# Dividing the first batch's softmax weights: by a diagonal in TensorE's turn, or row by row on GpSimd

## The chip, the cores and the metric

The kernel runs on one core of one Trainium2 chip. A core has five engines that run side by side, each with its own queue of instructions: TensorE (PE; its weight loads are listed as PEld) multiplies matrices into PSUM, VectorE (DVE) and ScalarE (ACT) work element by element and can read PSUM, GpSimd (POOL) works element by element in SBUF and issues some of the DMAs, SyncE (SP) issues the other DMAs. An engine takes its instructions strictly in order; a semaphore holds it where it needs another's result.

The metric is the device time of one execution in microseconds. The time before is 1459.56 us, the median of 3 runs (1455.29 to 1461.54).

## What is computed

A threshold attention, and behind it a two-layer block with the exact GELU. The attention keeps in each row only the scores that lie within tau of the row's largest, takes their exponentials, divides each row by its sum plus 1e-9, and weighs V with the result:

```python
batch, n_heads, seq, head_dim = (8, 8, 576, 64)            # q, k, v in FP32, tau = 0.02
scores = scale * np.matmul(q, k.transpose(0, 1, 3, 2))
thresh = np.max(scores, axis=-1, keepdims=True) - tau
scores = np.where(scores >= thresh, scores, -1000000000.0)
scores = scores - np.max(scores, axis=-1, keepdims=True)
attn = np.exp(scores)
attn = attn / (np.sum(attn, axis=-1, keepdims=True) + 1e-09)
attn_out = np.matmul(attn, v)
x = attn_out.transpose(0, 2, 1, 3).reshape(B * S, H * D)   # 4608 x 512
h = x @ w_in                                               # 512 x 2048
g = 0.5 * h * (1.0 + erf(h * inv_sqrt2))
out = g @ w_out                                            # 2048 x 512
```

`w_in` and `w_out` arrive in 64-bit floating point and are converted to FP32 by the kernel itself. Everything is computed in FP32.

## The kernel before

The heads are taken two at a time: a pair p is two heads of one batch, four pairs to a batch, 32 in all. The 576 rows of a pair's scores are cut into four chunks of 128 rows for each head and a fifth chunk that holds the last 64 rows of both heads. One pair and one chunk make a slot. A slot of chunk 0 to 3 works on two heads (n = 2 in the code, e = 0 and 1), a slot of chunk 4 on one tile. The main loop (L796) walks the slots, and within a slot the instructions of all engines are written out by hand in a fixed order; no scheduler reorders them.

Batch 0 (p below EARLY = 4) has 20 slots and is walked in two passes: chunks 0 and 1 of the four pairs (slots 0 to 7), then chunks 2, 3 and 4 of each pair (slots 8 to 19). What a slot of batch 0 does, in the order of the loop:

- `scores` (L351, matmuls L360): scores into the two PSUM buffers of the tag "sc". Each buffer comes free when the slot before has masked its scores (L391).
- `softmax_head` (L363): for each head the row maximum on DVE (L372, `nmx`), the threshold on POOL (L373, `thr`), the exponentials on ACT (L375, into `w`, a tile named p).
- `gelus`, `weigh_v`, `fill`, `table`: from slot 9 on, a part of the two-layer block's matmuls (L524) fills TensorE, and ACT does their GELUs (L503), which need another function table than the exponential: a table load before, and one behind (L510). `weigh_v` (L466) multiplies the turned weights with V, and ACT copies the result (L482).
- `turn_p_early` (L294) of the slot before: TensorE turns the 128x576 weights of each head, in 128-column pieces (L304) and 64-column remainders (L306), into PSUM buffers of the tag "mm" (four, shared with all other matmuls), and ACT copies them out (L314, L324; for chunk 4 DVE, L317 and L329).
- `softmax_tail` (L378): DVE sets to zero what is under the threshold and sums the rest in one instruction (L391), which needs scores, threshold and exponentials. POOL adds 1e-9 to the sum of each head (L394).
- `turn_qk_early` (L262) in slots 0, 2 and 4: Q and K of the next pair are turned.
- the conversions and the division. `conversions` (L162) turns the 32 pieces of the two weight matrices from 64 bits to FP32: on DVE `expo` (L179), `mant` (L186), `power` (L188) and the product (L190), on ACT `power` (L180); then `load_piece` (L140) lets POOL issue two DMAs (L157, L159) for a further piece. `convert(ns)` issues conversion steps until a debt of so many nominal nanoseconds is paid: 0 in slot 0, 3400 in slots 1 to 7, 3650 in slots 8 to 18, all that is left in slot 19. Of this share, 700 ns come first; then `divide_early` (L398): a reciprocal of the sums on DVE (L402), and on POOL one multiplication of a head's 128x576 weights by it, in place (L405); then the rest of the share.

So the next slot's thresholds (L373) stand on POOL behind this slot's multiplications and behind the DMA issues of this slot's pieces, and the next slot's maxima (L372) stand on DVE behind this slot's conversions.

From batch 1 on, weights are turned by DVE and DMAs and the division is done on the product with V (`divisors`, L407); the SBUF buffer of its divisors has the tag "inv" in the pool `dg`, one buffer. TensorE has the two-layer block to work on in all the time that attention leaves.

Of the kernel before, what the change touches and what calls it, by code (L numbers as in the profile page):

```python
# [8 lines left out]
FP32 = mybir.dt.float32  # L9
U32 = mybir.dt.uint32  # L10
U8 = mybir.dt.uint8
AF = mybir.ActivationFunctionType
ALU = mybir.AluOpType
# [5 lines left out]
def kernel(  # L19
# [28 lines left out]
    nc = tc.nc  # L48
    ctx.enter_context(tc.manual_schedule())

    B, H, S, D = q.shape
    d_model, d_ff = moe_w_in.shape
    P = 128
    Q = 32
    HP = H // 2
    NP = B * HP
    EARLY = HP
# [28 lines left out]
    dg = ctx.enter_context(tc.tile_pool(name="dg", bufs=1))  # L86
# [5 lines left out]
    ident = const.tile([P, P], FP32, name="ident")  # L92
# [105 lines left out]
    def convert(ns):  # L198

        if conv["steps"] is None:  # L200
            conv["steps"] = conversions()
        conv["debt"] += ns
        while conv["debt"] > 0:
            took = next(conv["steps"], None)
            if took is None:
                return
            conv["debt"] -= took
# [85 lines left out]

    def turn_p_early(p, i):  # L294

        s = st[p]
        if i == 0 or (p < HP and i == 2):
            s["pT"] = [one.tile([P, KR, S], FP32, tag=f"pT{e}", name=f"pT{e}") for e in range(2)]
        w = s.pop(("p", i))
        n = 1 if i == NC else 2  # L300

        def turn(to, cols, e):
            if cols.stop - cols.start == P:
                nc.tensor.transpose(to, w[:, cols], ident)  # L304
            else:
                nc.tensor.matmul(to, lhsT=w[:, cols], rhs=ident, start=True, stop=True)  # L306

        for e in range(n):
            tr = ps.tile([P, NC, P], FP32, tag="mm", name="tr")
            for c in range(NC):  # L310
                at = e * (S + TAIL) + c * P
                turn(tr[:, c, :], slice(at, at + P), e)
            if i < NC:
                nc.scalar.copy(s["pT"][e][:, 0:NC, i * P:(i + 1) * P], tr)  # L314
        if i == NC:
            for e in range(2):
                nc.vector.tensor_copy(s["pT"][e][:, 0:NC, MAIN:S], tr[:, :, e * TAIL:(e + 1) * TAIL])  # L317
        tails = s["pT"][0][:, NC, :]
        tr = ps.tile([P, NC, P], FP32, tag="mm", name="tr")
        if i < NC:  # L320
            for e in range(2):
                at = MAIN + e * TAIL
                turn(tr[e * TAIL:(e + 1) * TAIL, 0, :], slice(at, at + TAIL), e)
            nc.scalar.copy(tails[:, i * P:(i + 1) * P], tr[:, 0, :])  # L324
            return
        turn(tr[0:TAIL, 0, :], slice(MAIN, S), 0)
        for e in range(2):
            rows = slice(e * TAIL, (e + 1) * TAIL)
            nc.vector.tensor_copy(tails[rows, MAIN:S], tr[0:TAIL, 0, rows])  # L329
# [21 lines left out]
    def scores(p, i):  # L351
        s = st[p]
        n = 1 if i == NC else 2
        sc = s["sc", i] = [ps.tile([P, 2, 512], FP32, tag="sc", name="sc", bufs=2) for _ in range(n)]
        for h in range(2):
            for e in range(n):
                rows = slice(0, P) if i == NC else slice(e * D, (e + 1) * D)
                lhsT = s["q_tail"] if i == NC else s["qT"][rows, i * P:(i + 1) * P]
                at = h * HALF + (TAIL if p < EARLY and e == 0 else 0)
                nc.tensor.matmul(  # L360
                    sc[e][:, h, 0:HALF], lhsT=lhsT, rhs=s["kT"][rows, at:at + HALF], start=True, stop=True)
# [16 lines left out]
    def softmax_tail(p, i):  # L378

        s = st[p]  # L380
        sc, thr, w = s.pop(("sc", i)), s.pop(("thr", i)), s["p", i]
        n = len(sc)
        if p < EARLY:
            pair = small.tile([P, 2], FP32, tag="den", name="den")
            den = [pair[:, e:e + 1] for e in range(n)]
        else:
            at = [e * NC + i if i < NC else 2 * NC for e in range(n)]
            den = [sums[p % 2][:, x:x + 1] for x in at]
        for e in range(n):
            row = w[:, e * S:(e + 1) * S].rearrange("p (h s) -> p h s", h=2)  # L390
            nc.vector.scalar_tensor_tensor(  # L391
                row, sc[e][:, :, 0:HALF], thr[:, e:e + 1], row, op0=ALU.is_ge, op1=ALU.mult, accum_out=den[e])
            if p < EARLY:
                nc.gpsimd.tensor_scalar(den[e], den[e], 1e-9, None, op0=ALU.add)  # L394
        if p < EARLY:
            s["sum", i] = pair[:, 0:n]

    def divide_early(p, i):  # L398

        s = st[p]  # L400
        den, w = s.pop(("sum", i)), s["p", i]
        nc.vector.reciprocal(den, den)  # L402
        for e in range(den.shape[1]):
            row = w[:, e * S:(e + 1) * S]
            nc.gpsimd.tensor_scalar(row, row, den[:, e:e + 1], None, op0=ALU.mult)  # L405

    def divisors(p):  # L407

# [89 lines left out]
    def gelus(left):  # L498

        while len(late) > left:  # L500
            g, j, hT = late.pop(0)
            t = gp.tile([P, 2, TOK], FP32, tag="g", name="g")
            nc.scalar.activation(t, hT, AF.Gelu)  # L503
            g[j - 1], g[j] = t[:, 0, :], t[:, 1, :]
            dirty[0] = True
# [270 lines left out]
    BATCH = HP * SLOTS  # L776
# [19 lines left out]
    for n in range(len(slots) + WEIGH + 1):  # L796
        p, i = slots[n] if n < len(slots) else divmod(n, SLOTS)
        early = p < EARLY
        last = slots[n - 1] if 0 < n <= len(slots) else None
        if p < NP:  # L800
            scores(p, i)
            softmax_head(p, i)
        elif n == len(slots):
            ext = weights_in()
        if not early or n % 2 == 0:
            gelus(0)
            table()
        made = []
        for args in due:
            weigh_v(*args)  # L810
        due = []
        if p > EARLY and i == WEIGH:
            made = [weigh_v(p - 1, h * HALF, (h + 1) * HALF) for h in range(2)]
        owed += (goal(n) - goal(n - 1)) * BLK_NS * (PARTS[i] if not early and p < NP else 1.0)
        if early:
            fill(owed, tokens)
            owed = 0.0
            table()
        if last and last[0] < EARLY and last[1] < NC:
            turn_p_early(*last)  # L820
        if p < NP:
            softmax_tail(p, i)
        if made:
            made[0]()
        if p < NP and not early:
            turn_p(p, i)
        if made:
            made[1]()
        if p < NP and not early:
            if i == 2:  # L830
                regroup(p, 1)
            if i > 2:
                regroup(p, i)
            if i == NC:
                divisors(p)
        if last and last[0] < EARLY and last[1] == NC:
            turn_p_early(*last)
        if p < HP - 1 and i == 0:
            turn_qk_early(p + 1)
            if p == 0:  # L840
                load_early(3)
                load_v_early(2)
                load_v_early(3)
            if p < 2:
                load_piece()
        if p < HP and i == NC and 0 < p < HP - 1:
            load(p + 3)
        if n == BATCH:
            for t in pd_tail:
                nc.gpsimd.memset(t[:, NB:4 * KR, :], 0.0)  # L850
        if p >= HP and i == 1 and p + 2 < NP:
            loads = load_steps(p + 2)
        if p >= HP:
            next(loads, None)
        if p >= HP - 1 and i == 2 and p + 1 < NP:
            turn_qk(p + 1)
        share = 0 if n == 0 else 3400 if n < 2 * HP else 3650 if n < BATCH - 1 else 1e9
        if early:
            convert(min(share, 700))
            divide_early(p, i)  # L860
            share -= min(share, 700)
        convert(share)
        if not early:
            lag[0] = 2 if p < NP else 0
            fill(owed, tokens)
            owed = 0.0
        if last and last[0] < EARLY:
            if last[1] == 1:
                due.append((last[0], 0, TOK))
            if last[1] == NC:  # L870
                due.append((last[0], TOK, S))
        if n == START - 1:
            tokens = TOK
        elif n == BATCH + 1:
            tokens = S
        elif p > EARLY and i == WEIGH and p % HP == 0:
            tokens = p // HP * S
            for n in AWAY:
                if n in x_blk and (n + 1) * TOK <= tokens:
                    put_away(n)  # L880
# [34 lines left out]
```

## Time and profile before

| | |
|---|---|
| median of 3 runs | 1459.56 us (1455.29 to 1461.54) |
| the profiled execution: its own time, and its span | 1455.29 us, 1453.4 us |
| busy in the span: PE, DVE, ACT, POOL | 1386.1, 908.4, 629.2, 463.2 us |
| busy in the first 192 us: PE, DVE, ACT, POOL | 141.0, 141.9, 104.3, 139.7 us |
| L405 on POOL (weights times reciprocal) | 36, 76.1 us |
| L304 on PE (transposes of 128 columns) | 144, 26.2 us |
| L306 on PE (64-column remainders, as matmuls) | 72 records, 10.0 us |
| first masking operation of batch 0, of batch 1 | 12.86 us, 191.92 us |

How to read it: the times of an engine add up what it was busy with, and several engines work at once, so no such time is by itself a part of the end time. Which work decides is seen in the waits: what an engine stood still for, and for how long. A matmul in FP32 shows as two records on PE, a transpose as one.

### The profile page before, as it was taken

The numbers are of one execution on the slowest core, as the hardware profiler recorded it, in microseconds if no ns is written. First come the engines' busy times: TensorE is split into PE (matmuls) and PEld (weight loads), VectorE is DVE, ScalarE is ACT, GpSimd is POOL, SyncE is SP. The second block draws the span as 40 slices with busy tenths as digits, with TensorE's granted clock in tenths as the row PEclk, the third lists the DMA queues.
The fourth block names the chain that finished last, engine by engine and source line by source line (L and its number), as shares of the span: only waits on it lengthen the run. The fifth ranks groups of instructions, "written<-read, shape, count | busy, mean of one in ns | idle before, by whom it ended". The sixth has DMA issues, their size and how long they took to land.

```text
span 1453.4 us, 19399 instructions
## 1 busy us (share of the span) xinstructions
PE 1386.1 (95%) x6400; PEld 949.2 (65%) x6400; DVE 908.4 (63%) x1796; ACT 629.2 (43%) x1004; POOL 463.2 (32%) x862
## 2 busy tenths in 40 slices
PE   6778799999999999999999999999999999999999
PEld 4455546647556475664755646657488888888887
DVE  5788777777777777777677767777755042132230
ACT  4546733625437256372453736628242141240320
POOL 6787643434434434344344334341000000000000
PEclk9689899999999999999999999999999999999999
DMA  9766538777777777877877877777600000001000
GB/s 235 225 206 221 186 69 160 132 146 143 140 152 131 140 143 143 159 132 138 153 139 153 164 136 144 134 149 127 114 16 8 22 1 23 22 1 48 11 4 26
DMA packets 451794, 167.04 MB, mean 115 GB/s; under 512 B 413296, under 2 KB 436400, under 8 KB 451696
## 3 DMA queue, kind: packets, MB, share of 16 engines
q1 hardware_dynamic: 425488, 108.65, 41.0%
q0 software_dynamic: 23808, 56.57, 13.4%
q8 instruction: 52, 0.85, 0.2%
q10 hardware_dynamic: 2400, 0.59, 0.2%
q14 instruction: 46, 0.38, 0.1%
HBM read 71.68 MB, written 11.47 MB: 57 GB/s over the span
## 4 chain that ended last, share of the span: by engine, by line
PE 80%; DVE 7%; POOL 4%; ACT 3%; DMA 2%; issue 2%; SPq 1%; DVEq 0%; ACTq 0%; POOLq 0%
PE bank L657 27%; PE o_ps L537 17%; PE hT L524 17%; PE sc L360 11%; PE xT L466 9%; POOL p L405 3%; DVE p L391 2%; ACT p L375 2%; DVE nmx L372 1%; DMA k<-in_k_dram 1%; DVE power L188 1%; DMA pT<-turned_p 1%; ACT L503 1%; DVE mant L186 0%; DVE expo L179 0%
## 5 line engine op out<-in xcount | busy, mean ns | idle before, releaser
L375 ACT ACTIVATE p<-sc,nmx 128x576 f32<-128x576 f32 x288 | 202.2, 739 | 416.9 <-DVE nmx L372 416.9
L524 PE MATMUL hT<-x,w_in 128*128 128x256 f32 x1280 | 298.5, 386 | 0.0
L537 PE MATMUL o_ps<-w_out,g 128*128 128x512 f32 x640 | 294.6, 603 | 0.0
L372 DVE TENSOR_REDUCE nmx<-sc 128x1 f32<-128x576 f32 x288 | 205.0, 748 | 126.5 <-PE sc L360 126.0
L524 PEld LDWEIGHTS hT<-x,w_in 128*128 128x128 f32 x1280 | 240.2, 191 | 58.5 <-issue 25.6
L391 DVE SCALAR_TENSOR_TENSOR p<-sc,thr,p 128x576 f32<-128x576 f32 x288 | 225.3, 816 | 79.3 <-ACT p L375 57.2
L373 POOL TENSOR_SCALAR thr<-nmx,tau_eff 128x1 f32<-128x1 f32 x288 | 84.9, 296 | 514.3 <-DVE nmx L372 511.9
L537 PEld LDWEIGHTS o_ps<-w_out,g 128*128 128x128 f32 x640 | 116.9, 190 | 140.7 <-issue 138.9
L360 PE MATMUL sc<-kT,qT 64*128 64x288 f32 x960 | 171.3, 439 | 7.2 <-DVE p L391 6.8
L466 PE MATMUL xT<-pT,v 128*64 128x288 f32 (+2 forms) x1280 | 166.4, 412 | 4.6 <-ACT g L503 3.2
L438 DVE STREAM_TRANSPOSE turned_p<-p 128x1152 f32<-128x1152 f32 x112 | 154.1, 1376 | 3.2 <-DVE x L484 0.2
L360 PEld LDWEIGHTS sc<-kT,qT 64*128 64x128 f32 x960 | 96.0, 190 | 91.5 <-issue 76.3
L466 PEld LDWEIGHTS xT<-pT,v 128*64 128x64 f32 x1280 | 91.6, 138 | 76.2 <-issue 15.2
L235 POOL DMA_DIRECT2D v<-in_v_dram x208 | 110.6, 535 | 10.3 <-issue 9.4
L657 PE MATMUL bank<-x,w_in 128*128 128x256 f32 x384 | 93.3, 379 | 0.0
L657 PE MATMUL bank<-w_out,unit 128*128 128x256 f32 x416 | 92.4, 379 | 0.0
L510 ACT ACT_TABLE_LOAD x71 | 91.1, 1283 | 1.3
L503 ACT ACT_TABLE_LOAD x71 | 91.1, 1283 | 1.3
L657 PEld LDWEIGHTS bank<-w_out,unit 128*128 128x128 f32 x416 | 79.0, 190 | 10.7
L405 POOL TENSOR_SCALAR p<-p,den 128x576 f32<-128x576 f32 x36 | 76.1, 2118 | 12.2 <-DVE den L402 12.0
L657 PEld LDWEIGHTS bank<-x,w_in 128*128 128x128 f32 x384 | 73.0, 190 | 10.3 <-issue 0.5
L226 POOL DMA_DIRECT2D q<-in_q_dram x104 | 70.7, 685 | 15.6 <-issue 14.7
(150 smaller groups left out, 1358.3 us busy)
## 6 DMA issues: line engine op xcount, KB each, us to landing
pT<-turned_p SPq DMA_DIRECT2D x448, 160.0 KB, 4.1
pT<-pd_tail SPq DMA_DIRECT2D x112, 80.0 KB, 3.2
q<-in_q_dram POOLq DMA_DIRECT2D x104, 72.0 KB, 3.0
k<-in_k_dram POOLq DMA_DIRECT2D x104, 72.0 KB, 3.2
inv<-turned SPq DMA_DIRECT2D x56, 128.0 KB, 3.8
v<-in_v_dram POOLq DMA_DIRECT2D x156, 40.0 KB, 3.4
out_dram<-o_sb SPq DMA_DIRECT2D x20, 256.0 KB, 4.3
raw<-in_moe_w_in_dram POOLq DMA_DIRECT2D x8, 512.0 KB, 4.8
```

Source lines behind the costliest of these rows:

```text
L235: eng.dma_start(t[r:P:4, e, 0:n, :], rows[:, r * KR:r * KR + n, :])
L360: nc.tensor.matmul(sc[e][:, h, 0:HALF], lhsT=lhsT, rhs=s["kT"][rows, at:at + HALF], start=True, stop=True)
L372: nc.vector.tensor_reduce(nmx[:, e:e + 1], sc, axis=AXIS.XY, op=ALU.max, negate=True)
L375: nc.scalar.activation(w[:, e * S:(e + 1) * S].rearrange("p (h s) -> p h s", h=2), sc, AF.Exp, bias=nmx[:, e:e + 1], scale=1.0)
L391: nc.vector.scalar_tensor_tensor(row, sc[e][:, :, 0:HALF], thr[:, e:e + 1], row, op0=ALU.is_ge, op1=ALU.mult, accum_out=den[e])
L405: nc.gpsimd.tensor_scalar(row, row, den[:, e:e + 1], None, op0=ALU.mult)
L438: nc.vector.transpose(turned_p[:, :, 0:NB, i * Q:(i + 1) * Q], w.rearrange("p (e b i) -> p e b i", e=2, i=Q))
L466: nc.tensor.matmul(xT[f, 0:hi - lo], lhsT=s["v"][:, e, c, :], rhs=pT[:, c, lo:hi], start=(c == 0), stop=(c == KR - 1))
L503: nc.scalar.activation(t, hT, AF.Gelu)
L524: nc.tensor.matmul(hT[:, j % 2, :], lhsT=w_in_sb[c][:, j * P:(j + 1) * P], rhs=x_blk[n][:, c, :], start=(c == 0), stop=(c == N_DM - 1))
L537: nc.tensor.matmul(o[:, 0:d_model], lhsT=g[j][:, m * P:(m + 1) * P], rhs=w_out_sb[j], start=(j == 0), stop=(j == N_DF - 1))
L657: nc.tensor.matmul(to, lhsT=l, rhs=r, start=start and k == 0, stop=k == len(pairs) - 1, skip_group_check=not start)
```

## The change

The weights of batch 0 are no longer multiplied by the reciprocal of their sum on POOL. Instead a diagonal matrix of the reciprocals is made for each head: ACT copies the identity, 128x128, with each row scaled by 1/sum. TensorE's turn, a transpose in 128-column pieces before and a matmul with the identity for the remainders, becomes a matmul with this diagonal for both, so that the weights come out turned and divided. The diagonals lie in one buffer (two heads, 128x128 each) of the tag "inv". The reciprocal on DVE now stands behind the slot's whole share of conversions, where it stood behind the first 700 ns of it. The addition of 1e-9 is one instruction for both heads. The order of instructions on the engines is otherwise the same; POOL has 20 rows fewer in the listing, with the DMA issues in the same order among themselves.

```diff
     def turn_p_early(p, i):
...
-        w = s.pop(("p", i))
+        w, diag = s.pop(("p", i)), s.pop(("diag", i))
         n = 1 if i == NC else 2
 
         def turn(to, cols, e):
-            if cols.stop - cols.start == P:
-                nc.tensor.transpose(to, w[:, cols], ident)
-            else:
-                nc.tensor.matmul(to, lhsT=w[:, cols], rhs=ident, start=True, stop=True)
+            nc.tensor.matmul(to, lhsT=w[:, cols], rhs=diag[:, e, :], start=True, stop=True)
...
             nc.vector.scalar_tensor_tensor(
                 row, sc[e][:, :, 0:HALF], thr[:, e:e + 1], row, op0=ALU.is_ge, op1=ALU.mult, accum_out=den[e])
-            if p < EARLY:
-                nc.gpsimd.tensor_scalar(den[e], den[e], 1e-9, None, op0=ALU.add)
         if p < EARLY:
+            nc.gpsimd.tensor_scalar(pair[:, 0:n], pair[:, 0:n], 1e-9, None, op0=ALU.add)
             s["sum", i] = pair[:, 0:n]
 
-    def divide_early(p, i):
+    def diagonal(p, i):
 
         s = st[p]
-        den, w = s.pop(("sum", i)), s["p", i]
+        den = s.pop(("sum", i))
+        n = den.shape[1]
         nc.vector.reciprocal(den, den)
-        for e in range(den.shape[1]):
-            row = w[:, e * S:(e + 1) * S]
-            nc.gpsimd.tensor_scalar(row, row, den[:, e:e + 1], None, op0=ALU.mult)
+        diag = s["diag", i] = dg.tile([P, 2, P], FP32, tag="inv", name="diag")
+        for e in range(n):
+            nc.scalar.activation(diag[:, e, :], ident, AF.Copy, bias=0.0, scale=den[:, e:e + 1])
...
-        share = 0 if n == 0 else 3400 if n < 2 * HP else 3650 if n < BATCH - 1 else 1e9
+        convert(0 if n == 0 else 3400 if n < 2 * HP else 3650 if n < BATCH - 1 else 1e9)
         if early:
-            convert(min(share, 700))
-            divide_early(p, i)
-            share -= min(share, 700)
-        convert(share)
+            diagonal(p, i)
```

## The prediction, made before the changed kernel was run

> **What bounds the kernel now.** I cut the span first at the start of the first masking operation (L391) of some of the twenty slots of batch 0 (n = 0 to 19): n = 0 starts at 12.86 us, n = 5 at 57.46, n = 9 at 94.16, n = 12 at 119.53, and the first slot of batch 1 at 191.92. Columns: stretch, its length, busy time of PE, PEld, DVE, ACT, POOL (instructions), granted PE clock, DMA share, GB/s.
>
> ```profile
> 12.86:57.46 44.60, 32.09 (x166) 21.03 (x166) 31.47 (x63) 25.66 (x53) 35.47 (x47) 0.77 0.89 241
> 57.46:94.16 36.70, 25.59 (x120) 15.06 (x120) 29.23 (x54) 15.59 (x30) 30.35 (x39) 0.67 0.55 179
> 119.53:191.92 72.39, 55.59 (x277) 37.71 (x278) 57.12 (x113) 48.66 (x78) 47.72 (x62) 0.91 0.54 176
> 191.92:1453.40 1261.48, 1245.13 (x5714) 856.09 (x5712) 766.57 (x1514) 524.98 (x822) 323.62 (x671) 1.00 0.53 101
> ```
>
> After 191.92 TensorE is busy 98.7% of the time, and the change touches nothing there. So the end moves by as much as 191.92 moves. Before it no engine is full, and POOL, which is nearly idle late, is as busy as DVE. The waits say who holds whom (us in total, times, longest):
>
> ```profile
> DVE p L391 <- POOL thr L373: 19.4, 12, 3.5
> ```
>
> ```profile
> PE tr L304 <- POOL p L405: 16.1, 14, 2.9
> ```
>
> The timeline of one slot shows the mechanism:
>
> ```profile
> 60.08 4.48 POOL L405 TENSOR_SCALAR p<-p,den 128x576 f32<-128x576 f32 x2 [0.39 <-DVE den L402]
> ...
> 62.86 1.42 DVE L372 TENSOR_REDUCE nmx<-sc 128x1 f32<-128x576 f32 x2
> ...
> 64.51 0.60 POOL L157 DMA_DIRECT2D raw<-in_moe_w_in_dram  x1
> ...
> 66.77 0.59 POOL L373 TENSOR_SCALAR thr<-nmx,tau_eff 128x1 f32<-128x1 f32 x2
> 67.13 0.82 DVE L391 SCALAR_TENSOR_TENSOR p<-sc,thr,p 128x576 f32<-128x576 f32 x1 [2.85 <-POOL thr L373]
> ```
>
> DVE has both maxima at 64.28. The thresholds that it needs next are queued on POOL behind two divisions (4.48 us) and four DMA issues that the divisions held back. DVE stands 2.85 us.
>
> **The change part by part.** *Removed: 36 divisions on POOL* (76.1 us at 2.12 us each). That gives two terms.
>
> (a) The wait for the threshold. Where POOL is free, DVE starts L391 0.28 us after the second maximum (five such slots, and 191.92), so that much stays: 19.4 - 12 x 0.28 = 16.0 us, plus 1.0 of one wait of 1.3 that is booked on another releaser while thr ended just before it. 17.0 us.
>
> (b) DVE's conversions are slowed while a division runs. These two rows are the same operation:
>
> ```profile
> 89.30 0.69 DVE L190 SCALAR_TENSOR_TENSOR w_in<-mant,power 128x512 f32<-128x512 uint32 x1
> 97.10 1.12 DVE L190 SCALAR_TENSOR_TENSOR w_in<-mant,power 128x512 f32<-128x512 uint32 x1
> ```
>
> Of the 128 operations of L179, L186, L188 and L190, 40 are slow by some 0.4 us, and 38 of these lie on a division. Busy time less 32 times the fast duration: 17.5 - 32 x 0.42, 17.7 - 32 x 0.41, 26.0 - 32 x 0.68 and 26.1 - 32 x 0.69, 4.0 to 4.6 each, 16.8 us. All of it is in DVE's order ahead of the next maximum.
>
> Together 33.8 us, the most that DVE's own chain can give. By slot (wait above 0.28 plus slow excess) it is 23.5 in n = 1 to 11 and 10.3 in n = 12 to 19.
>
> (c) *Not realised in n = 12 to 19.* There the ScalarE chain runs beside it:
>
> ```profile
> 145.20 1.37 ACT L375 ACTIVATE p<-sc,nmx 128x576 f32<-128x576 f32 x2 [1.41 <-DVE nmx L372]
> 146.97 1.28 ACT L503 ACT_TABLE_LOAD   x1
> 148.88 1.28 ACT L510 ACT_TABLE_LOAD   x1
> 150.28 1.05 ACT L314 COPY pT<-tr 128x512 f32<-128x512 f32 x2
> 150.90 0.44 PE L306 MATMUL tr<-ident,p 128*64 128x128 f32 x4 [1.27 <-ACT pT L314]
> 151.27 2.14 PE L360 MATMUL sc<-pd_tail,q_tail 128*128 128x288 f32 x4
> 153.45 0.76 DVE L372 TENSOR_REDUCE nmx<-sc 128x1 f32<-128x576 f32 x1 [1.21 <-PE sc L360]
> ```
>
> Exponentials, two table loads around a GELU, copies, the last turned columns, scores, next maximum: 0.75 + 1.4 + 3.4 + 0.5 + 0.6 + 0.45 + 1.25 + small gaps = 8.6 us with two heads, 7.5 with one. POOL is not in it. Maximum to maximum was 8.7, 9.4, 9.9, 9.1, 7.2, 12.0, 11.4 and 6.1 us from n = 12 on. The first, fourth, fifth and seventh are this chain; of the 10.3 I keep 4.5 (1.1 at n = 13, 0.95 at 14, 0.3 at 15, 1.2 at 17, the rest at 16, 18 and 19), so -5.8.
>
> (d) *TensorE: 144 transposes become FP32 matmuls with a diagonal.* The trace of before has no FP32 matmul of 128 columns by 128. What it has:
>
> ```profile
> L304 PE MATMUL tr<-ident,p 128*128 128x128 f32 x144 | 26.2, 317 | 25.4 <-POOL p L405 16.1 <-POOL den L394 5.4 <-issue 1.8
> L306 PE MATMUL tr<-ident,p 128*64 128x128 f32 x72 | 10.0, 339 | 6.0 <-ACT pT L314 3.7 <-DVE pT L317 1.0 <-ACT x L482 0.7
> ```
>
> L304's 144 turns left one record each, a row of eight lasting 1.09 us, 0.109 apart at full clock. L306's 36 turns, matmuls already, left two records each. So a matmul is two records. Lower bound: 2 x 0.109 = 0.218 us, weight load hidden as in L524 (128x256, records 0.216 apart). Upper bound: no overlap, load and stream of 0.109 each twice, 0.436. Records of L304 and L524 both start as soon as the last ended, so I take 0.218: 144 x 0.109 = +15.7 us of PE at full clock, 0.87 per slot with two heads. TensorE is idle 51 us of the first 192, by the table above 12.5 and 11.1 of them in the nine slots from 12.86 to 94.16, 2.6 a slot, which covers 0.87. It does not where fill work and V meet at n = 9 to 12. There scores 1.9 + fill 3.4 + turns 2.2 = 7.5 us stand against 6.9 on DVE: -1.4 us. If the cover were gone, all 15.7 would count.
>
> The Trainium skill ("TensorE: Matmul & The Clock Gate", Terms) says that the transpose mode is four times faster for FP32, which speaks against the change: by it the 144 turns would cost 3 x 0.109 x 144 = 47 us more, about all of the idle time, and the gain would be gone. L306's two records, not four, are against it.
>
> (e) *Half clock.* Between 25 and 90 us TensorE's granted clock is about half in four stretches, 44 us together (0.52 from 58.8 to 72.4, for instance). In one, scores 3.0 + turns 16 x 0.213 + 0.7 = 7.1 us, 10.4 with V (3.3), against 6.9 on DVE. Some two of the eight slots would show it: from 0 (the matmuls keep the clock up) to -7, I take -2.
>
> The same page (Part 4: PE-mode transpose) says that transposes do not count as activity for the clock gate. The drop near 59 us came after 6.7 us in which TensorE was busy 5.0, of them 1.7 in turns; that fits the rule but does not prove it. By this rule (e) is 0 or a small gain.
>
> (f) *ScalarE: 36 copies of the identity scaled by 1/den.* Nearest row: L324, 128x128, 0.286 us; 10.3 us together. They run after the reciprocal, beside the 1.41 us of the next two maxima on the DVE, for which the next exponential waits anyway. Cost 0; uncovered, 0.6 per slot. Bounds 0 and -10.
>
> (g) *The reciprocal moves behind the whole share of conversions.* Nothing on DVE is longer; the diagonal comes 4.4 us after L391's end (3.5 conversions, 0.2, 0.7), where the second division ended 5.5 us after it (64.56 against 59.0). The single diagonal buffer makes ScalarE wait for the turns of the slot before, which stand ahead of the scores that the next exponential needs anyway: 0.
>
> (h) *POOL:* 1e-9 added once for both heads, 16 instructions of 0.33 less; the DMA issues of L157 and L159 are no longer behind a division, so a piece is asked for up to 2.5 us earlier. DMA share is 0.89 up to 57 us, so two waits of DVE for landings (1.4 and 1.7) stay. 0.
>
> Sum: 33.8 - 5.8 - 1.4 - 2.0 = 24.6; for slots that now have no slack left on DVE I take off 1.6 more, as one late score among sixteen is likely: 23. The profiled execution (span 1453.4, 1455.29 us) would then take 1432. The median shown is 4.27 above it: 1459.56 - 23 = **1437 us**.
>
> **The rivals.** *TensorE becomes the bound (slower).* For: FP32 turns at 0.436 add 47 us to 141 busy in 192. With some 20 us that cannot be filled (11.5 before the first scores, the first V), the stretch lasts 141 + 47 + 20 = 208: 1459.6 + 16 = 1476 us. It decides from 0.32 us per turn, where 141 + 31 + 20 = 192. Against: the two records. 11%.
>
> *No change.* The first eleven slots go from POOL to half-clocked TensorE and late diagonals, 9 us each as now; (c) alone is left, 4.5 less: 1455 us. For: clock 0.67 with 70% busy. Against: TensorE idles before every transpose now, for POOL. 13%.
>
> *All of it.* Clock full, ScalarE chain shortened by faster scores: 33.8 + 2: 1424 us. 8%.
>
> **How the numbers follow.** The likeliest, 68%: 1437. Its unknowns: (e) 0 to -7, (f) 0 to -10, (c) 0 to -10, so 1426 to 1452 by itself. The range reaches to the no-change case: 1424 to 1457. 0.5% (7 us) is about what a measurement tells here. Faster: the first and third case and a little of the second, 0.77; same 0.12; slower 0.11.
>
> **What would show it.** Right: L391's wait for thr gone; L188 and L190 at 0.69; the turns at two records, 0.109 apart; slots 1 to 11 near 7 us; the first slot of batch 1 near 169 us; the same 1261 us behind it. Wrong: turn records 0.2 apart at full clock, TensorE full before 190 us, or maxima waiting for scores in slots 1 to 8.

## The result, and the profile after

The changed kernel takes 1433.28 us (median of 4 runs, 1432.31 to 1435.96); the kernel before, run beside it, 1458.12 us. The ratio is 0.9832 with a 95% interval of 0.9805 to 0.9858: 1.7% faster. The forecast was 1437, with 1424 to 1457 as its range. (The changed file has fewer lines: L391 of before is L389 after, L372 is L370, L373 is L371, L375 is L373, L405 is gone and L403 is the new diagonal.)

The same table of stretches as before, now for the changed kernel: from the first masking operation to that of slot 12, from there to the first of batch 1, and the rest. Columns: stretch, length, busy time of PE, PEld, DVE, ACT, POOL, granted clock, DMA share, GB/s.

```profile
12.85:100.56 87.71, 73.53 (x467) 55.37 (x468) 71.84 (x160) 56.94 (x119) 37.62 (x76) 0.92 0.90 271
100.56:169.28 68.72, 58.28 (x338) 43.24 (x336) 51.45 (x114) 53.87 (x92) 19.59 (x43) 0.98 0.54 180
169.28:1431.80 1262.52, 1246.92 (x5720) 856.25 (x5718) 766.76 (x1514) 525.03 (x822) 323.57 (x671) 1.00 0.53 101
```

Batch 1 starts at 169.28 us in place of 191.92, 22.6 earlier, and what follows lasts 1262.5 us in place of 1261.5. The span of the profiled execution is 21.6 us shorter; the medians differ by 24.8. So the whole gain lies in batch 0, as the prediction had it. Slots 0 to 11 went from 106.7 to 87.7 us, slots 12 to 19 from 72.4 to 68.7.

Who waits for whom in the first 170 us, first DVE, then TensorE:

```profile
DVE nmx L370 <- PE sc L358: 16.7, 7, 7.0
DVE p L389 <- ACT p L373: 10.1, 21, 1.8
DVE mant L186 <- ACT power L180: 4.4, 2, 3.5
DVE expo L179 <- DMA raw<-in_moe_w_in_dram: 3.5, 1, 3.5
```

```profile
PE tr L304 <- ACT diag L403: 13.5, 7, 3.1
```

The wait for the thresholds, 19.4 us, is no longer in the list; what masking waits for is the exponential, in 13 of 21 cases some 0.2 us, 1.8 at the longest. TensorE's wait for POOL became a wait for the diagonal, which will matter below. The groups that answer to those shown of before:

```profile
L304 PE MATMUL tr<-diag,p 128*128 128x128 f32 x288 | 41.9, 302 | 18.5 <-ACT diag L403 13.5 <-ACT g L501 4.3 <-ACT x L480 0.7
L403 ACT ACTIVATE diag<-ident,den 128x128 f32<-128x128 f32 x36 | 12.6, 393 | 7.8 <-DVE den L400 7.8
L188 DVE SCALAR_TENSOR_TENSOR power<-raw,power 128x512 uint32<-128x512 uint32 x16 | 10.9, 683 | 0.1
L190 DVE SCALAR_TENSOR_TENSOR w_in<-mant,power 128x512 f32<-128x512 uint32 x16 | 11.1, 691 | 0.5
```

288 records for 144 turns: two each. These two groups of conversion steps run at 0.68 and 0.69 us, where their means were 0.83 and 0.87.

The length of each slot, from one first masking operation to the next, in us. The last two columns are variants from the experiments (their first series). Slot 0 has the same order of instructions in the changed kernel and with the early diagonal, and the changed kernel, profiled a second time (experiment 10), took 7.81 us in slot 1 and 11.29 in slot 2: differences of about 1 us in slots 0 to 2 are not to be read as effects.

| slot | before | changed | early diagonal | and earlier piece |
|---|---|---|---|---|
| 0 | 7.28 | 7.56 | 6.15 | 7.47 |
| 1 | 8.66 | 7.00 | 6.94 | 6.94 |
| 2 | 10.51 | 10.27 | 10.51 | 6.55 |
| 3 | 9.88 | 6.90 | 6.84 | 6.84 |
| 4 | 8.28 | 8.54 | 6.54 | 6.54 |
| 5 to 11, mean | 8.87 | 6.78 | 6.72 | 6.72 |
| 12 to 19, mean | 9.05 | 8.59 | 8.68 | 8.68 |
| batch 1 starts at | 191.92 | 169.28 | 166.20 | 163.72 |

### The profile page after: what moved, and what is told of

Its sections match the earlier page's. It is cut to its first block, busy times and chain, and to the rows that moved or that the text cites. A ratio compares the mean times of both kernels' runs of the same rounds, so it can differ in the third digit from the quotient of the medians.

```text
span 1431.8 us, 19665 instructions
## 1 busy us (share of the span) xinstructions
PE 1384.7 (97%) x6544; PEld 959.2 (67%) x6544; DVE 892.2 (62%) x1796; ACT 640.4 (45%) x1040; POOL 387.6 (27%) x810
## 4 chain that ended last, share of the span: by engine, by line
PE 78%; DVE 8%; ACT 4%; DMA 4%; SPq 3%; issue 2%; POOL 0%; DVEq 0%; ACTq 0%; POOLq 0%
PE bank L655 27%; PE hT L522 16%; PE o_ps L535 15%; PE sc L358 11%; PE xT L464 8%; SPq L452 2%; DVE p L389 2%; ACT p L373 2%; DVE nmx L370 1%; PE tr L304 1%; DMA k<-in_k_dram 1%; DMA inv<-turned 1%; DVE power L188 1%; DMA turned<-turned 1%; SPq L448 1%
## 5 line engine op out<-in xcount | busy, mean ns | idle before, releaser
L373 ACT ACTIVATE p<-sc,nmx 128x576 f32<-128x576 f32 x288 | 202.4, 739 | 394.4 <-DVE nmx L370 394.3
L370 DVE TENSOR_REDUCE nmx<-sc 128x1 f32<-128x576 f32 x288 | 204.7, 748 | 138.1 <-PE sc L358 137.9
L389 DVE SCALAR_TENSOR_TENSOR p<-sc,thr,p 128x576 f32<-128x576 f32 x288 | 225.3, 816 | 65.9 <-ACT p L373 65.1
L371 POOL TENSOR_SCALAR thr<-nmx,tau_eff 128x1 f32<-128x1 f32 x288 | 84.7, 294 | 556.6 <-DVE nmx L370 554.7
L358 PE MATMUL sc<-kT,qT 64*128 64x288 f32 x960 | 167.0, 435 | 4.1 <-DVE p L389 3.8
L655 PEld LDWEIGHTS bank<-x,w_in 128*128 128x128 f32 x384 | 73.0, 190 | 10.3 <-issue 0.5
L304 PE MATMUL tr<-diag,p 128*128 128x128 f32 (+1 forms) x360 | 50.6, 307 | 22.5 <-ACT diag L403 13.5
```

What stands on the lines that cost most here:

```text
L358: nc.tensor.matmul(sc[e][:, h, 0:HALF], lhsT=lhsT, rhs=s["kT"][rows, at:at + HALF], start=True, stop=True)
L370: nc.vector.tensor_reduce(nmx[:, e:e + 1], sc, axis=AXIS.XY, op=ALU.max, negate=True)
L373: nc.scalar.activation(w[:, e * S:(e + 1) * S].rearrange("p (h s) -> p h s", h=2), sc, AF.Exp, bias=nmx[:, e:e + 1], scale=1.0)
L389: nc.vector.scalar_tensor_tensor(row, sc[e][:, :, 0:HALF], thr[:, e:e + 1], row, op0=ALU.is_ge, op1=ALU.mult, accum_out=den[e])
L655: nc.tensor.matmul(to, lhsT=l, rhs=r, start=start and k == 0, stop=k == len(pairs) - 1, skip_group_check=not start)
```

## The experiments

Two theories stood against each other. A: POOL's division cost the time, because the next thresholds queued behind it and because it slowed DVE's conversions. B: the clock did it, since matmuls keep TensorE at full speed where transposes let it drop. Each run is compared with runs of the kernel before on the same chip.

**1. Only TensorE's half of the change.** In the kernel before:

```diff
-            if cols.stop - cols.start == P:
-                nc.tensor.transpose(to, w[:, cols], ident)
-            else:
-                nc.tensor.matmul(to, lhsT=w[:, cols], rhs=ident, start=True, stop=True)
+            nc.tensor.matmul(to, lhsT=w[:, cols], rhs=ident, start=True, stop=True)
```

> The kernel before, with only TensorE's half of the change: the 144 turns are FP32 matmuls with the identity, the division stays on POOL. Theory A (the gain is POOL's: the thresholds' wait of 17 us and the slowed conversions of 17 us): L391 still waits some 19 us for thr, the conversions stay slow, and the time stays within 6 us of the kernel before, 1458 (1455 to 1464). Theory B (the gain is the clock's: granted half speed fell from 61.6 to 17.3 us because turns now count as matmuls): the clock in the first 192 us rises from 0.84 to 0.9 or more and the time falls by 10 us or more, to 1436 to 1448.

Measured: 1454.95 us, ratio 0.9993 (0.9977 to 1.0008). The first 192 us of this run:

```profile
0.00:192.00 192.00, 149.97 (x829) 108.14 (x830) 141.05 (x282) 103.66 (x182) 138.98 (x191) 0.91 0.68 203
```

And masking still waits for the thresholds (L388 and L370 in this file):

```profile
DVE p L388 <- POOL thr L370: 21.8, 14, 3.4
```

The clock rose from 0.84 to 0.91 and TensorE's busy time from 141.0 to 150.0, and nothing was gained. Theory B falls: DVE and TensorE were waiting for POOL all the same. It also shows that the dearer turns cost nothing where POOL is the bound.

**2. Only the thresholds off POOL.** In the kernel before:

```diff
-            nc.gpsimd.tensor_scalar(
+            (nc.vector if p < EARLY else nc.gpsimd).tensor_scalar(
                 thr[:, e:e + 1], nmx[:, e:e + 1], -1.0, tau_eff, op0=ALU.mult, op1=ALU.subtract)
```

> The kernel before, with batch 0's 36 thresholds on VectorE, so that they no longer stand behind the divisions on POOL; division and transposes stay. Theory A: the wait for thr (19 us) is gone, the slowed conversions (16.8 us) stay, 36 operations of about 0.15 us come to VectorE, and TensorE still waits for the divided weights: 1445 to 1452. Theory B: no clock is won, so no gain: 1455 to 1462. If the threshold wait was only the place where POOL's own load showed (4.4 divisions + 2.3 DMA issues a slot), the gain is under 4 us.

Measured: 1450.04 us, ratio 0.996 (0.9942 to 0.9979). Batch 1 starts at 182.5 in the profiled execution, 9.4 us earlier, and the medians differ by 6.3. The predicted 17.0 us of waits less 36 thresholds of 0.214 us (7.7) on DVE would be 9.3. The conversions stay slow (17.2 us above their fast time, by the same sum as in the prediction) and slots 3 to 11 still take 7.2 to 8.9 us; TensorE still waits for the divided weights, 14.8 us. So the wait is real, and taking it away is a part of the gain, not all.

**3. No division at all.** In the changed kernel (the division of batch 0 is left out):

```diff
-        diag = s["diag", i] = dg.tile([P, 2, P], FP32, tag="inv", name="diag")
-        for e in range(n):
-            nc.scalar.activation(diag[:, e, :], ident, AF.Copy, bias=0.0, scale=den[:, e:e + 1])
```

and the turns are the transposes of before.

> The changed kernel without the division of batch 0: no diagonals, and the turns are transposes again; the reciprocals are computed and not used. It prices what the change put in place of POOL's division (15.7 us of TensorE, 12.6 us of ScalarE). Theory A: both lie mostly beside other work: 1426 to 1433, 0 to 7 us under the changed kernel. Theory B: the transposes bring the half clock back (over 40 us of it), and the time is above the changed kernel's: 1440 or more.

Measured: 1428.64 us, ratio 0.9803 (0.9785 to 0.9822), some 5 us under the changed kernel. All that the change put in POOL's place costs some 5 us (4.0 at the start of batch 1). Next to experiment 4 this becomes sharper. The first 192 us of this run:

```profile
0.00:192.00 192.00, 157.60 (x778) 100.01 (x778) 146.43 (x322) 114.53 (x198) 76.56 (x166) 0.92 0.73 216
```

The half clock did not come back, as theory B had expected it to: with the transposes of before the clock is 0.92 (over the slots of batch 0 alone 0.90, where it was 0.83 before and 0.91 in experiment 1). Taking the division off POOL raised it about as much as experiment 1 did with the division in place. So the low clock of before was not the transposes' doing alone; it went along with TensorE's waits for POOL.

**4. The diagonal earlier.** In the changed kernel, reciprocal and diagonal go where the reciprocal was before:

```diff
-        convert(0 if n == 0 else 3400 if n < 2 * HP else 3650 if n < BATCH - 1 else 1e9)
+        share = 0 if n == 0 else 3400 if n < 2 * HP else 3650 if n < BATCH - 1 else 1e9
         if early:
+            convert(min(share, 700))
             diagonal(p, i)
+            share -= min(share, 700)
+        convert(share)
```

> The changed kernel with reciprocal and diagonals behind the first 700 ns of a slot's conversions, where the reciprocal stood before. Theory A: TensorE's 13.5 us of waits for the diagonal go, but VectorE's order is just as long and bounds slots 1 to 11: 0 to 4 us faster, 1429 to 1433. If the late diagonal was part of the bound (my step that it costs 0 being wrong), 6 us or more faster: 1427 or less.

Measured: 1428.03 us, ratio 0.9808 (0.9779 to 0.9836). It lies between the two expectations, and its interval overlaps that of the changed kernel; experiment 10 settles the difference. With the diagonals early the kernel is as fast as with no division at all (1428.64), as far as these spreads of 3 and 8 us tell: the 144 dearer turns and the 36 copies on ScalarE are then covered, and what the change lost was the price of having the diagonal late. Slot 4 shows how. The timeline of the changed kernel, start and length in us:

```profile
43.12 0.69 ACT L403 ACTIVATE diag<-ident,den 128x128 f32<-128x128 f32 x2 [1.07 <-DVE den L400]
...
43.58 3.71 PE L304 MATMUL tr<-diag,p 128*128 128x128 f32 x20 [2.99 <-ACT diag L403]
...
47.22 0.91 PE L278 MATMUL tr<-ident,q 128*128 128x128 f32 x4
...
48.17 0.69 ACT L281 ACTIVATE qT<-tr,q_scale 128x512 f32<-128x512 f32 x1 [0.57 <-PE tr L278]
...
49.90 1.42 DVE L370 TENSOR_REDUCE nmx<-sc 128x1 f32<-128x576 f32 x2 [0.95 <-PE sc L358]
50.34 1.33 ACT L180 ACTIVATE power<-expo,rebias 128x512 uint32<-128x512 uint32 x2
...
51.58 0.68 ACT L403 ACTIVATE diag<-ident,den 128x128 f32<-128x128 f32 x2
...
52.28 1.37 ACT L373 ACTIVATE p<-sc,nmx 128x576 f32<-128x576 f32 x2
...
53.12 0.82 DVE L389 SCALAR_TENSOR_TENSOR p<-sc,thr,p 128x576 f32<-128x576 f32 x1 [1.80 <-ACT p L373]
```

TensorE stands 2.99 us for the diagonal of slot 3. Behind the turn, on TensorE, are the turns of the next pair's Q and K; behind those, on ScalarE, their copies, then the conversions' `power`, then the next diagonal, then the next exponential, for which masking waits 1.80 us. The next scores are late too: the maxima wait 0.95 us for them. The same stretch with the early diagonal (this view begins at 41 us; the turn itself began at 39.83):

```profile
40.64 2.64 PE L304 MATMUL tr<-diag,p 128*128 128x128 f32 x17
...
43.21 0.66 PE L278 MATMUL tr<-ident,q 128*128 128x128 f32 x4
...
48.91 1.37 ACT L373 ACTIVATE p<-sc,nmx 128x576 f32<-128x576 f32 x2
...
49.75 0.82 DVE L389 SCALAR_TENSOR_TENSOR p<-sc,thr,p 128x576 f32<-128x576 f32 x1 [0.64 <-ACT p L373]
```

Q is turned 4.0 us earlier, of which the slots before had brought 1.4, and slot 4 lasts 6.54 in place of 8.54.

**5. POOL's work back, with nobody reading it.** The kernel of experiment 4, and behind the reciprocal of slots 0 to 16 two multiplications (one in the slots of chunk 4) that write a weight tile not yet in use. The tile that they read is set to 1 once, at the start:

```diff
         nc.vector.reciprocal(den, den)
+        if p < 3 or i < 2:
+            for e in range(n):
+                nc.gpsimd.tensor_scalar(w_out_sb[14], w_out_sb[15], den[:, e:e + 1], None, op0=ALU.mult)
```

> The kernel with the early diagonal (1428.03 us), with two multiplications of 128x512 on POOL put back where the division stood, in slots 0 to 16; nothing reads their result. Theory A (POOL's presence costs, by the thresholds queued behind it and by slowing conversions): about 15 x 0.35 us of wait and some 14 us of slowed conversions in the covered slots come back, 15 to 25 us: 1443 to 1453, with some 30 slow conversions. Theory C (POOL cost only because TensorE needed its result): the time stays at 1426 to 1432.

Measured: 1450.67 us, ratio 0.9968 (0.9953 to 0.9983), 22.6 us above experiment 4. DVE's wait is back:

```profile
DVE p L390 <- POOL thr L372: 18.7, 12, 3.0
```

and 31 conversion steps are slow, 11.9 us together, all beside one of the 31 multiplications (9 of these slowed none, 12 two or three). Nobody needs what POOL makes here. Its presence in the queue and beside DVE is the cost: theory A holds, and C falls, by which POOL cost only because TensorE needed its result.

**6. The same elements in four times as many instructions.**

```diff
-            for e in range(n):
-                nc.gpsimd.tensor_scalar(w_out_sb[14], w_out_sb[15], den[:, e:e + 1], None, op0=ALU.mult)
+            for k in range(4 * n):
+                at = slice(k % 4 * P, (k % 4 + 1) * P)
+                nc.gpsimd.tensor_scalar(w_out_sb[14][:, at], w_out_sb[15][:, at], den[:, k // 4:k // 4 + 1], None, op0=ALU.mult)
```

> The same with eight multiplications of 128x128 for the two of 128x512: the same number of elements in four times as many instructions. If VectorE is slowed once for each POOL instruction (38 slow operations for 36 divisions), there are about four times as many slow conversions as with two, over 80, and the time lies above that run's by 5 us or more. If it is slowed for as long as POOL is busy, the number of slow conversions stays near that run's and the times agree within 4 us plus what the extra instructions add to POOL.

Measured: 1473.83 us, ratio 1.0132 (1.0113 to 1.0152). Neither expectation is met. The groups of POOL's multiplications, first of experiment 5, then of this one:

```profile
L404 POOL TENSOR_SCALAR w_out<-w_out,den 128x512 f32<-128x512 f32 x31 | 60.8, 1962 | 6.7 <-DVE den L401 5.1
```

```profile
L405 POOL TENSOR_SCALAR w_out<-w_out,den 128x128 f32<-128x128 f32 x124 | 92.2, 758 | 5.3 <-DVE den L401 5.2
```

Two stretches of the timeline, the first while DVE stands, the second beside conversion steps up to 69.5 us:

```profile
59.89 2.92 POOL L405 TENSOR_SCALAR w_out<-w_out,den 128x128 f32<-128x128 f32 x5
...
66.89 5.42 POOL L405 TENSOR_SCALAR w_out<-w_out,den 128x128 f32<-128x128 f32 x7 [0.30 <-DVE den L401]
```

The conversions are hardly slow (3.1 us above their fast time in all, for 124 instructions), though they overlap POOL's multiplications about as long as in experiment 5 (43 against 46 us). So the slowing is neither a price for each instruction nor one for each busy microsecond. Here it is POOL that is slowed: the 47 multiplications that overlap a conversion step take 1.02 us in the mean, the other 77 take 0.60. The time is lost at the thresholds: four short multiplications take 3.0 us where one long one took 2.0, and the wait for thr grows from 18.7 to 52.2 us.

**7. The slowing without the wait.** Experiment 5 with the thresholds of batch 0 on DVE, as in experiment 2.

> The two multiplications of 128x512 on POOL put back (as in the run that gave 1450.67 us), with batch 0's thresholds on VectorE, so that they wait for nothing on POOL. The slowed conversions (11.9 us of excess there) stay, and 36 thresholds of 0.2 us come to VectorE. Theory A (slowed conversions cost in their own right): 1428 + 12 + 7 = 1447, 1442 to 1450. If only the threshold wait cost: 1428 + 7 = 1435, 1432 to 1437.

Measured: 1438.85 us, ratio 0.9873 (0.9853 to 0.9892), against 1429.39 for the early diagonal in the same series: 9.5 us more, between the two expectations. Of 11.6 us of slow conversions and 7.7 us of thresholds added to DVE half shows at the end and two thirds at the start of batch 1, which is 13.0 us later. So of the 22 us in experiment 5 the slowing by itself can be at most about half. How the wait and the slowing share exactly is left open.

**8. No table loads.** The kernel of experiment 4, with the GELUs of batch 0's slots as plain copies (the first block's GELU is left out):

```diff
-            nc.scalar.activation(t, hT, AF.Gelu)
+            if in_first[0]:
+                nc.scalar.copy(t, hT)
+            else:
+                nc.scalar.activation(t, hT, AF.Gelu)
...
-            dirty[0] = True
+            dirty[0] = not in_first[0]
```

> The kernel with the early diagonal, with the GELUs of batch 0's slots replaced by copies, which need no table load (the GELU of the first block is left out). Theory A (my step c: in slots 12 to 19 the chain over ScalarE's table loads bounds, not POOL or VectorE): slots 12 to 18, now 7.1 to 11.8 us, shorten by 5 to 12 us together: 1416 to 1423. If VectorE or the turns bound them: within 3 us of 1428.

Measured: 1418.81 us, ratio 0.9754 (0.9736 to 0.9773), 9.2 us under experiment 4 (7.9 by the two ratios, as the chips differ). Slots 12 to 19, first of experiment 4 and then of this one:

```profile
96.80:166.20 69.40, 61.24 (x348) 45.50 (x347) 51.52 (x113) 53.66 (x92) 19.51 (x44) 0.98 0.55 181
```

```profile
97.64:157.90 60.26, 58.72 (x348) 44.23 (x347) 51.12 (x113) 34.12 (x71) 19.45 (x44) 1.00 0.67 209
```

ScalarE loses 19.5 us of work, 18.0 of them 14 table loads, and the stretch 9.1, and TensorE is then busy 97% of it. So in slots 12 to 19 the chain over the table loads is the bound, and TensorE comes right behind it.

**9. The fourth weight piece earlier.** The kernel of experiment 4:

```diff
-            if p < 2:
-                load_piece()
+            if p == 0:
+                load_piece()
+                load_piece()
```

> The kernel with the early diagonal, with the fourth weight piece asked for in slot 0 in place of slot 2. If the 4.0 us wait of VectorE for this landing in slot 2 comes from the late request: 2 to 4 us faster, 1424 to 1426. If it is DMA bandwidth (share 1.03 up to 51 us), the wait moves and the time stays at 1426 to 1430.

Measured: 1426.85 us, ratio 0.9811 (0.9793 to 0.9828). DVE's wait of 4.0 us in slot 2 is gone (10.51 to 6.55 us), and no other wait of DVE for a piece takes its place, so it was the late request, not bandwidth. But slot 0 was 1.3 us longer in this execution, so slots 0 to 2 together gave 2.6, and the end did not move clearly. So the three were run once more, together on one chip.

**10. The three again.**

> The changed kernel again, as it stands, beside the two variants below on one chip: 1431 to 1436.

> The early diagonal again. If the late diagonal costs what the first look said: 3 to 6 us under the changed kernel of this series, 1427 to 1430. If that difference was one of chips: within 2 us of it.

> Early diagonal and earlier fourth piece again. Its first slot of batch 1 stood 2.5 us earlier than with the early diagonal alone, its end only 0.2 us. If the 2.5 us are real: 1425 to 1427 and under the early diagonal by 1 to 3 us; if slot 0's 1.3 us (landing of K) and the tail eat them: within 1 us of it.

Measured: 1435.78 us for the changed kernel (ratio 0.9857, 0.9837 to 0.9876), 1429.39 with the early diagonal (0.9806, 0.9785 to 0.9827), 1424.76 with the earlier piece too (0.9777, 0.9759 to 0.9794). The early diagonal is worth 6 us, clear of both intervals. The earlier piece adds 4.6 here after 1.2 in the first series, and its interval overlaps the other's; in both series batch 1 starts 2.2 to 2.5 us earlier with it. The last version beats both the kernel before and the changed one.

## Why the prediction was right, point by point

**The frame.** "The end moves by as much as 191.92 moves": 22.6 us there, 21.6 at the end of the profiled execution. Right.

**(a) and (b), 17.0 and 16.8 us.** Both went in full: DVE's waits for thr come to 0.2 us in all, and the excess of the conversions fell from 17 to about 1 us. Experiments 1 and 5 show that POOL was the cause. In one point the sum was kinder than its terms: (b) by itself reaches the path only in part (experiment 7). (a) by itself brought about its 17.0 less the price on DVE at the start of batch 1, 9.4 against 9.3, but 6.3 at the end (experiment 2).

**By slot.** For slots 1 to 11 the prediction had 23.5 less 5 of deductions, 18.5; they gave 19.2. For slots 12 to 19 it kept 4.5 of 10.3; they gave 3.7. Step (c), the ScalarE chain as the bound there, is shown by experiment 8.

**(d) 0.218 us per turn, +15.7 us.** Two records per turn, and at full clock they start 0.112 us apart, so 0.224. The weight load is hidden. The figure of the Trainium skill ("TensorE: Matmul & The Clock Gate", Terms), transposes four times faster in FP32, does not fit this case: it is a factor of two. The rival that rested on 0.436 is out. Slots 5 to 11 take 6.78 us, and 6.59 in experiment 3, where the turns are the cheaper transposes, so at most 0.2 us of such a slot is the price of the turns.

**(e) -2 us for half clock.** The granted clock over the slots of batch 0 rose from 0.83 to 0.95 (means of the stretches, weighted by their lengths), so the loss did not come. The skill's rule that transposes are not counted as activity (same page, Part 4: PE-mode transpose) agrees with experiment 1, where only the kind of turn differs and the clock goes from 0.84 to 0.91. But experiment 1 does not prove the rule, since the turns also last twice as long there, and the rule is not the whole account: in experiment 3 the clock is 0.92 with transposes. Experiment 1 also shows that the clock by itself is worth nothing while POOL's division is in place.

**(f) ScalarE's diagonals, cost 0.** One takes 0.393 us, not 0.286: a copy with a scale per row costs 0.1 more than a plain one, as the rows of before could have told (L281 with 0.69 us, L283 with 0.59, both 128x512). At 12.6 us in all they are covered when they come early, as experiment 4 against 3 shows within its spread.

**(g) The late reciprocal, cost 0.** This is the step that was wrong in size: 5 to 6 us at the end, 3.1 and 4.2 us at the start of batch 1 in the two series. Of these, 2.0 us lie in slot 4 in both; slots 0 to 2 differ by as much from one execution to the next, and why the two kernels also differ by 4.0 and 1.0 us behind batch 0, where they are the same, is not explained. The prediction compared the diagonal's time with the end of the second division, 4.4 against 5.5 us, and stopped there. It did not name what stands behind the turn in slots 2 and 4, the turns of the next Q and K and their copies, and behind these the next exponential. (Only slot 4 shows the price; slot 2 is held by the landing of a piece.) With the wait at the thresholds gone there was no slack left to hide it. One of the prediction's own signs of being wrong did appear, maxima that wait for scores in slots 1 to 8: 0.95 us for slot 5 and 0.38 for slot 7 (slot 1's 3.8 was there before, with 3.6); with the early diagonal both are gone. That the sum still came out near, 23 predicted and 22.6 measured in batch 0, is luck in part: the 1.6 us taken off "for slots that now have no slack left" and the 2 us of (e) that did not come stood in for (g).

**(h) Two waits for landings stay.** They became one, 3.5 us where there were 3.1. Right as a size; the reason given, bandwidth, was wrong, as experiment 9 shows.

## What to carry to other kernels

An engine that is busy a third of the whole time can be the bound of a stretch, when short instructions that others need stand in its queue behind long ones: look for what a wait's releaser was doing just before, not for its share of the span. When such a wait goes, everything that was hidden under it comes to light, so a step that the change moves later has to be followed to the last instruction queued behind it on every engine. And a moved instruction is cheap to try in two places: here its place was worth a quarter as much as the change itself.

## What the runs showed of the hardware

A long multiplication on POOL (128x576, 2.12 us) slows some of the conversion steps that run beside it on DVE: of the 86 steps that lay on one of the 36 divisions, 38 were slow, by some 0.43 us. In experiment 5, 31 of the 71 beside a multiplication of 128x512 were slow, by some 0.37 us. Short ones (128x128) hardly slow DVE: 124 of them cost it 3.1 us. There POOL pays: 1.02 us for one beside a conversion step, 0.60 without. The row maxima (L372), which read PSUM, were not slowed: 20 beside a division took 0.747 us, 18 others 0.743 (medians). Masking (L391) stayed at 0.81 us, but none of it ran beside a division.

Multiplications on POOL with no conversion step beside them took 0.60 us (128x128), 1.58 (128x512, three of them) and 1.76 (128x576, two). By the first two, one costs an estimated 0.27 us plus 2.6 ns per column ((1.58 - 0.60) / 384), so cutting it up is dear.
